# The last key block of a backward attention sweep, moved from beside a recurrent chain to between weight-gradient matmuls

## The chip, the cores and the metric

The kernel runs on one core of one Trainium2 chip. The metric is the device time of one execution in microseconds. Three runs of the kernel before gave a median of 5579.31 us (5578.82 to 5591.48).

## What is computed

The program is the forward pass and all gradients of a gated mix of two layers over 2048 tokens of width 576. Cut to what matters:

```python
g = sigmoid((x * gate_w).sum(-1))
# A: 32 query heads of 18 columns that share one key and one value head
p = softmax(q_h @ k.T * 18 ** -0.5);  a = concat(p @ v) @ wo
# B: 64 segments of 32 tokens; 8 memory rows go from one segment to the next
for s in range(64):
    h = concat([mem, x[32 * s:32 * s + 32]])
    q, k, v = h @ Wq, h @ Wk, h @ Wv            # 32 heads of 128 columns
    o = (masked_softmax(q @ k.T * 128 ** -0.5) @ v) @ Wo
    mem = o[:8];  out_B[s] = o[8:]
out = g * a + (1 - g) * out_B
# and the gradients of out in x, wq, wk, wv, wo, mem0, Wq, Wk, Wv, Wo and gate_w
```

The change concerns two parts of the backward pass: the gradients of A's one key and one value head, and B's recurrence run backward. It also concerns the weight gradients of B, which come after both. What is computed stays the same.

## The kernel before

The engines each run their own instructions in order and wait for each other through semaphores. Between the first stages and the end the order is the order of the code: `manual_schedule` is on, and two Python generators are woven by hand. `Kern.weave` runs a sweep and a chain side by side: a few leading sweep steps, then after every `yield` of the chain one sweep step, or more where the dictionary `extra` says so for the number of that yield. What follows is named **piece** for the stretch of chain between two yields, and **segment** for the chain's work on one of B's 64 segments.

**The sweep** (`a_pass2`) makes A's key and value gradients. It goes over 4 blocks of 512 keys (kb); for each over 16 pairs of heads and 16 tiles of 128 queries, so 256 steps a block, 1024 in all, each for one **pair** of heads. Step n issues:

- two matmuls for the scores of step n + 1 into `b_S` (two PSUM banks, one buffer of this kind), on 32 rows of TensorE each,
- two matmuls for dP of step n into two of three `b_dP` banks, on 32 other rows each,
- ACT's exponential of `b_S` into `b_E` (L1801), and DVE's product of `b_dP` and `b_E` into `b_dS` (L1824), in two halves,
- four matmuls of step n - 1 that add into `b_acc`, on 32 columns of TensorE each.

So `b_S` of the next step can be filled only after the exponential has read it. Queries come as `b_QS` from `qs_dram`, 256 KB for four steps (L1782), keys as `b_KV`, once a block. At a block's end ACT copies `b_acc` into a tile of the `b_dS` kind (L1837), and POOL stores it in `dkv_dram` (L1839).

**The chain** (`b_chain_bwd`) goes backward over the 64 segments. A segment depends on the one after it through `dm`, the gradient of the memory rows. Its 16 pieces are, in order: three for the projection of `dm` with WoT (two halves of 20 matmuls, 32 columns of TensorE each, into the banks `r_pj` and `r_x`); one for transposes (`mem_T`) and the dv gradient (`mem_grad`); one for the score gradients (`pd`, then `dS` on DVE); ten that share 48 `heads` **units** of four matmuls of 288 columns (`r_pj` from `WT` and `r_dT`), two of them with the other two `mem_grad` calls, and the last of them with the copies `r_hp` on ACT (L1167) and `r_hs` on DVE (L1168); and one for the row sums `pm`, which give the next `dm` (L1185).

Beside this, the chain makes B's dk and dv of the upper 11 of 16 token tiles in 176 **key/value units** (`kv_load`, `kv_mm`, `kv_out`): eight matmuls into `r_x`, a copy on ACT (L1035), a store on POOL (L1036). Four units ride in each of the 5th to the 48th segments, each copied one piece after its matmuls. `load_dT` (L973) reads such rows back, transposed, for later segments. Nearly all loads are issued by SP's queue, in the order of the code.

`weave` gives the sweep 12 leading steps and eight extra ones at each of the pieces 4, 7 and 10; with one step a piece for 16 x 64 = 1024 pieces the sweep ends in the 62nd segment, and the last two segments run alone.

**The weight gradients** (`b_dw`) come after `b_post`. `groups` yields groups of matmuls that contract over 20 tiles of 128 rows into `w_acc` (six PSUM banks): for k < 4 the output is dWo (pairs of accumulators of 288 columns), then dWq, dWk and dWv (512 columns). Copies alternate between DVE and ACT (L77, L79). Between the groups stand transposes of `mem_tok` (banks `z_pt`) and one `gate` for each k, with a row of DVE operations (L909 to L920).

Of the kernel before, what the change touches and what calls it, by code (L numbers as in the profile page):

```python
# [36 lines left out]
KVT = 11  # L37
RIDE = 24
# [8 lines left out]
class Kern:  # L47
# [529 lines left out]
    def mem_tok(self, wi, sp, psum, nb):  # L577
# [10 lines left out]
        for mt in range(n):  # L588
# [9 lines left out]
            for h8 in range(4):  # L598
                pt = psum.tile([P, 8, P], BF16, name="z_pt", bufs=nb)
# [298 lines left out]
    def gate(self, tt, L, wo, sp, psum):  # L898
# [3 lines left out]
        pa = [psum.tile([P, 512], F32, name="w_acc", bufs=6) for _ in range(2)]  # L902
# [27 lines left out]
    def b_chain_bwd(self, wot, sp, kd, kvp, keep, psum):  # L930
# [86 lines left out]
        def kv_mm(n):  # L1017
# [4 lines left out]
            pk = psum.tile([P, 4, P], F32, name="r_x", bufs=1)  # L1022
# [22 lines left out]
        for s in reversed(range(NSEG)):  # L1045
# [3 lines left out]
            n0 = 4 * (NSEG - 1 - s - 4)  # L1049
# [3 lines left out]
            pj = [psum.tile([P, 512], F32, name=nm, bufs=1) for nm in ("r_pj", "r_x")]  # L1053
            for k, parts in enumerate((((0, (0, 1, 2)),), ((0, (3, 4)), (1, (0,))), ((1, (1, 2, 3, 4)),))):
                for j, kts in parts:
                    self.proj_part(pj[j], d_, self.WoT, j, kts)
                    if kts[-1] == 4:
                        self.evac(dOm[:, 4 * j:4 * j + 4, :].rearrange("p u e -> p (u e)"), pj[j][:], use="s")
                if k == 1:
                    x_rows(s, 0, pT[:, 0, :])  # L1060
                yield
# [24 lines left out]
            pg = mem_grad("r_pj", ((rows(mrow["dx"], E), [perm] * 8), (rows(dOm), blk(PqB))))  # L1086
            yield
# [14 lines left out]
            mem_cols(2, pg)  # L1102
# [3 lines left out]
            self.expand(dSB[:], dS[:].rearrange("p a (u q) -> p (a u) q", q=8), 16)  # L1106
            yield
# [12 lines left out]
            heads(2)  # L1120
            kv_mm(n0)
# [4 lines left out]
            kv_out(n0)  # L1126
# [12 lines left out]
            yield  # L1139
            heads(2)  # L1140
            kv_mm(n0 + 1)
            nc.gpsimd.dma_start(self.dTm_dram[s // 16][:, :, s % 16, :], dTc[:].rearrange("p w u c t -> p w (u c t)"))
            yield
            kv_out(n0 + 1)
            heads(7)
            load_dT(s - 1, 2)
            if s:
                pad_in("p", nxt["pT"][:, 1, :])
            yield
            heads(7)  # L1150
            if s:
                load_c(s - 1)
            yield
            heads(2)
            kv_mm(n0 + 2)
            if s:
                Pq = pad_T("p")
            yield
            kv_out(n0 + 2)
            heads(7)  # L1160
            load_dT(s - 1, 0)
            if n0 == -4:
                kv_load(0)
            yield
            heads(7)
# [4 lines left out]
            if n0 == -4:  # L1170
                kv_load(1)
# [3 lines left out]
            kv_mm(n0 + 3)  # L1175
# [137 lines left out]
    def b_dw(self, sp, wA, wB, wH, psum):  # L1313
# [3 lines left out]
        WS = ("o", "dq", "dk", "dv")  # L1317

# [24 lines left out]
        def groups(k, ts, ht):  # L1343
            if k < 4:
                od = self.outs[10].rearrange("h e d -> (h e) d")
                for t, cs in ts:
                    for i in range(4):
                        acc = [psum.tile([P, 512], F32, name="w_acc", bufs=6) for _ in range(2)]
                        for it in range(n):
                            for hf in range(2):  # L1350
                                self.mm(acc[hf][:, 0:288], lhsT=t[:, it, 128 * i:128 * i + 128],
                                        rhs=ht[:, it, 288 * hf:288 * hf + 288], start=(it == 0), stop=(it == n - 1))
                        o16 = sp.tile([P, D], BF16, name="w_o16b", bufs=3)
                        for hf in range(2):
                            self.evac(o16[:, 288 * hf:288 * hf + 288], acc[hf][:, 0:288])
# [5 lines left out]
            for t, cs in ts:  # L1361
                for kt in range(4):
                    acc = psum.tile([P, 512], F32, name="w_acc", bufs=6)
# [7 lines left out]
            acc = psum.tile([P, 512], F32, name="w_acc", bufs=6)  # L1371
# [10 lines left out]
        with self.tc.manual_schedule():  # L1382
# [6 lines left out]
            mem = None  # L1389
            for k in range(16):  # L1390
                ts = nxt
                if k % 4 == 0 and k < 12:
                    mem = self.mem_tok(k // 4, sp, psum, 2)
                    next(mem)
# [5 lines left out]
                if k == 15:  # L1400
                    self.final_load(wA, wH)
# [7 lines left out]
            pg = [psum.tile([P, 512], F32, name="w_acc", bufs=6) for _ in range(2)]  # L1409
# [354 lines left out]
    def a_pass2(self, keep, sp, psum):  # L1764
# [4 lines left out]
        def load_KV(kb):  # L1769
            if kb < 4:  # L1770
                KV[kb] = keep.tile([P, 512], BF16, name="b_KV", bufs=2)
                nc.sync.dma_start(KV[kb][:], self.kv_dram[:, kb * 512:kb * 512 + 512])

        load_KV(0)
        Q, S, E_, D_ = {}, {}, {}, {}
        NC = 4 * NPR * NTT // 4

        def load(c):
            if c < NC:
                p, q4 = (c // 4) % NPR, c % 4  # L1780
                QS = sp.tile([P, 2, 512], BF16, name="b_QS", bufs=3)
                nc.sync.dma_start(QS[:], self.qs_dram[p, q4])  # L1782
                Q[c] = (QS[:, 0, :], QS[:, 1, :].rearrange("p (a b) -> p a b", b=P))

        def pair(n):
            return n // (NPR * NTT), n // 4, n % 4
# [22 lines left out]
        NP_ = 4 * NS  # L1809
        for n in range(NP_ + 1):  # L1810
            if n < NP_:
                if n % 4 == 2:
                    load(n // 4 + 2)
                if n % NS == NS // 2:
                    load_KV(n // NS + 1)
                if n + 1 < NP_:
                    mm_S(n + 1)
                dP = [psum.tile([P, 512], F32, name="b_dP", bufs=3) for _ in range(2)]
# [6 lines left out]
            if n > 0:  # L1825
# [9 lines left out]
                if o % NS == NS - 1:  # L1835
                    dkv = sp.tile([P, 2, 512], BF16, name="b_dS", bufs=2)
                    nc.scalar.copy(dkv[:, 0, :], acc[:])  # L1837
                    k0 = (o // NS) * 512
# [266 lines left out]
```

## Time and profile before

| what | value |
| --- | --- |
| median of 3 runs | 5579.31 us |
| span of the profiled execution | 5569.0 us, 204829 instructions |
| median less span (no time of the profiled execution alone is recorded) | 10.3 us |
| PE / DVE / ACT / POOL busy | 94% / 67% / 63% / 41% |
| chain and sweep together, first to last r_hp and the lead | 2814.1 to 4523.4 us |
| `b_post` up to the wait ahead of the weight gradients | about 4525 to 4774 us |
| weight gradients | 4788.6 to about 5466 us |
| final stage | about 5470 to 5569 us |

Times in the profile are in us unless marked ns. PE is TensorE's matmuls, PEld its weight loads, DVE VectorE, ACT ScalarE, POOL GpSimd, SP SyncE. A row of a timeline has the start from the span's beginning, the time from the first start to the last end, engine, line, operation, output and input, how many in a row, and in brackets the idle time before and who ended it. A row of the windows view has the stretch, its length, the busy time of PE, PEld, DVE, ACT and POOL with instruction counts, the granted TensorE clock (1.00 is full), the busy share of the 16 DMA engines, and GB/s. A row of the waits view has the engine, what waited and for whom, the total, how many times, and the longest. Ends of matmuls are modelled, so two matmuls that run together or follow each other closely both show about 0.39 us; their starts are the better measure. The helper `mm` is L82, so matmuls are told apart by their tiles.

### The profile page before, as it was taken

To read this page: it belongs to the slowest core of one execution; us is meant where nothing else is said; L and a number is where in the kernel's file an instruction comes from. 1 tells how busy PE (TensorE), PEld (TensorE's weight loads), DVE (VectorE), ACT (ScalarE), POOL (GpSimd) and SP (SyncE) were. 2 spreads that over 40 slices of the span, in tenths; PEclk is the share of its full clock that TensorE was granted. 3 is DMA by queue.
4 is the path that set the end of the run, shared out by engine and by line. 5 is a ranking of instruction groups with operands and counts; after the bars stand their busy time and mean duration, and the time that the engine had idled before them with its cause. 6 is when DMAs were issued, how large, how long until landed. Compare 5 with 4: busy or idle time off the path is not lost. (4 is left out here: it accounts for less than half of the span.)

```text
span 5569.0 us, 204829 instructions
## 1 busy us (share of the span) xinstructions
PE 5231.2 (94%) x87117; PEld 2909.5 (52%) x87117; DVE 3726.0 (67%) x6818; ACT 3506.8 (63%) x5266; POOL 2297.4 (41%) x4320
## 2 busy tenths in 40 slices
PE   7999999999999998999969999999998889899999
PEld 6434444444444445777734555555544457674444
DVE  5337888888888887888868888888888821121111
ACT  4327888788878886888857878878877732111101
POOL 4004555555555545555514544444543421122213
PEclk9999999999999998999979999999999999999999
DMA  6646666766675546888765999999987679876653
GB/s 214 220 173 136 136 138 137 137 138 133 144 135 117 119 99 192 258 256 253 233 228 156 199 200 208 213 202 212 215 181 146 138 181 250 244 214 229 209 165 115
DMA packets 1109896, 1012.49 MB, mean 182 GB/s; under 512 B 666386, under 2 KB 919067, under 8 KB 1099378
## 3 DMA queue, kind: packets, MB, share of 16 engines
q1 hardware_dynamic: 1004706, 747.39, 56.4%
q0 software_dynamic: 100736, 247.10, 14.4%
q8 instruction: 681, 11.16, 0.9%
q10 hardware_dynamic: 3536, 4.90, 0.3%
q14 instruction: 237, 1.94, 0.1%
HBM read 547.90 MB, written 383.13 MB: 167 GB/s over the span
## 5 line engine op out<-in xcount | busy, mean ns | idle before, releaser
L1684 DVE TENSOR_TENSOR a_W<-a_dP,a_E 128x512 bf16<-128x512 f32 x2048 | 1315.1, 684 | 269.9 <-issue 128.7
L1824 DVE TENSOR_TENSOR b_dS<-b_dP,b_E 128x512 bf16<-128x512 f32 x2048 | 1311.8, 684 | 249.3 <-issue 109.0
L1801 ACT ACTIVATE b_E<-b_S 128x1024 bf16<-128x1024 f32 x1024 | 1048.3, 1024 | 308.2 <-PE b_dP L82 237.0
L1654 ACT ACTIVATE a_E<-a_S 128x1024 bf16<-128x1024 f32 x1024 | 1050.0, 1025 | 255.8 <-PE a_dP L82 166.5
L82 PEld LDWEIGHTS <-b_QS 32*128 32x128 bf16 (+1 forms) x8192 | 258.0, 92 | 564.9 <-issue 521.4
L82 PE MATMUL r_pj<-WT,r_dT 128*32 128x288 bf16 x12288 | 496.7, 289 | 17.0 <-issue 16.5
L82 PE MATMUL b_S<-b_KV,b_QS 32*128 32x512 bf16 x2048 | 409.1, 390 | 96.8 <-ACT b_E L1801 77.7
L82 PE MATMUL w_acc<-w_d,w_h 128*128 128x512 bf16 (+1 forms) x2400 | 473.8, 379 | 0.0
L82 PE MATMUL a_S<-a_QD,l_KV 32*128 32x512 bf16 x2048 | 400.3, 384 | 39.5 <-ACT a_E L1654 34.9
L82 PE MATMUL b_acc<-b_dS,b_QS 128*32 128x512 bf16 x2048 | 430.8, 399 | 0.7 <-DVE b_dS L1824 0.5
L82 PE MATMUL b_dP<-b_KV,b_QS 32*128 32x512 bf16 x2048 | 409.8, 394 | 8.2 <-DVE b_dS L1824 8.2
L82 PE MATMUL a_acc<-a_W,l_WK 128*32 128x512 bf16 x4096 | 414.5, 390 | 2.7 <-issue 2.4
L82 PE MATMUL b_acc<-b_E,b_QS 128*32 128x512 bf16 x2048 | 412.8, 400 | 0.0
L82 PE MATMUL a_acc<-a_E,l_VK 128*32 128x512 bf16 x4096 | 405.0, 381 | 5.8 <-issue 1.1
L82 PE MATMUL a_dP<-a_QD,l_KV 32*128 32x512 bf16 x2048 | 399.2, 386 | 0.0
L82 PEld LDWEIGHTS <-r_dT 128*32 128x32 bf16 x12288 | 333.8, 97 | 114.8 <-issue 24.0
L82 PEld LDWEIGHTS <-w_h 128*128 128x128 bf16 (+1 forms) x2688 | 229.8, 100 | 258.8 <-issue 6.9
L82 PEld LDWEIGHTS <-hm 128*32 128x32 bf16 x7680 | 203.9, 97 | 195.0 <-issue 0.8
L769 POOL TENSOR_TENSOR x_P<-x_E,x_r 128x512 bf16<-128x512 bf16 x128 | 152.7, 1193 | 293.6 <-DVE x_r L766 293.6
L79 ACT CAST w_o<-w_acc 128x512 bf16<-128x512 f32 x54 | 31.6, 585 | 384.3 <-PE w_acc L82 365.0
L77 DVE CAST w_o<-w_acc 128x512 bf16<-128x512 f32 x54 | 37.3, 691 | 333.4 <-PE w_acc L82 306.5
L82 PEld LDWEIGHTS <-l_KV 32*128 32x128 bf16 x4096 | 122.0, 91 | 250.6 <-issue 206.2
(461 smaller groups left out, 10953.2 us busy)
## 6 DMA issues: line engine op xcount, KB each, us to landing
b_QS<-qs_dram SPq DMA_DIRECT2D x256, 256.0 KB
dOx_dram<-p_tok SPq DMA_DIRECT2D x16, 1024.0 KB
c_vx<-vx_dram SPq DMA_DIRECT2D x64, 256.0 KB
krow_dram<-c_k POOLq DMA_DIRECT2D x64, 256.0 KB
qrow_dram<-c_q POOLq DMA_DIRECT2D x64, 256.0 KB
vrow_dram<-c_v POOLq DMA_DIRECT2D x64, 256.0 KB
x_q<-qx_dram SPq DMA_DIRECT2D x32, 512.0 KB
x_dO<-dOx_dram SPq DMA_DIRECT2D x32, 512.0 KB
```

Of the source, the lines that this page charges most:

```text
L77: nc.vector.tensor_copy(out, in_)
L79: nc.scalar.copy(out, in_)
L82: return self.nc.tensor.matmul(out, lhsT, rhs, start=start, stop=stop, tile_position=tp, skip_group_check=True)
L769: nc.gpsimd.tensor_tensor(out=o[:, r, :], in0=Et[:, :, lo:lo + n], in1=rl[:].unsqueeze(2).to_broadcast([P, 4, n]), op=ALU.mult)
L1654: nc.scalar.activation(E_[n][:], S.pop(n)[:], ACT.Exp, scale=SCALEA)
L1684: nc.vector.tensor_tensor(out=W_[n][:, i, :], in0=dP[i][:], in1=E_[n][:, i, :], op=ALU.mult)
L1801: nc.scalar.activation(E_[n][:], S.pop(n)[:], ACT.Exp, scale=SCALEA)
L1824: nc.vector.tensor_tensor(out=D_[n][:, i, :], in0=dP[i][:], in1=E_[n][:, i, :], op=ALU.mult)
```

## The change

- The sweep is cut. Key blocks 0 to 2 (768 steps) stay beside the chain. Block 3 becomes a second generator in `b_dw`: six steps ahead of all groups, then one step whenever `weave` there has counted 4800 more columns of `w_acc` matmuls, inside the groups; what is left would be run at k = 15. This second sweep has pools of its own, two `b_dP` banks in place of three, and its loads go out on ACT's queue.
- `w_acc` has three banks in place of six, and `z_pt` shares them. For k < 4 the two halves of an output are made one after the other.
- The chain has 12 pieces a segment in place of 16. The projection is in two pieces of a whole half each; the score gradients, the heads and the loads are spread anew.
- Key/value units: four in each of the 5th to 16th segments, then three up to the 59th. The first of a segment stands behind the score gradients in bank `r_pj`, with its copy in the same piece; the others are copied in the same piece too, but for the last.
- `extra` gives eight more steps at the pieces 4, 6 and 7, and one fewer, that is none, at the first piece of each of the 5th to 40th segments. Lead, pieces and extras make 768 steps.
- The block-end copy uses a tile of the units' kind (`r_kvo`) in place of a `b_dS` tile.

```diff
+        def kv_first(s):
+            q = NSEG - 1 - s - 4
+            return 4 * q if q < KV4 else 4 * KV4 + 3 * (q - KV4)      # KV4 = 12
...
-            for k, parts in enumerate((((0, (0, 1, 2)),), ((0, (3, 4)), (1, (0,))), ((1, (1, 2, 3, 4)),))):
...
+            for j, nm in enumerate(("r_pj", "r_x")):
+                pj = psum.tile([P, 512], F32, name=nm, bufs=1)
+                self.proj_part(pj, d_, self.WoT, j, range(NKT))
+                self.evac(dOm[:, 4 * j:4 * j + 4, :].rearrange("p u e -> p (u e)"), pj[:], use="s")
...
             self.expand(dSB[:], dS[:].rearrange("p a (u q) -> p (a u) q", q=8), 16)
+            kv_mm(n0, "r_pj")
+            kv_out(n0)
             yield
...
-            heads(2)
-            kv_mm(n0)
+            heads(4)
+            kv_mm(n0 + 1)
...
-            kv_out(n0)
+            kv_out(n0 + 1)
             heads(8)
...
-            heads(3)
+            heads(4)
+            load_dT(s - 1, 2)
             mem_cols(0, mem_grad("r_x", ((rows(L["kx"]), blk(dSB)), (rows(mrow["k"]), blk(dSB, 8)))))
             yield
-            heads(3)
             mem_cols(1, mem_grad("r_x", ((rows(mrow["dx"]), [perm] * 8), (rows(mrow["q"]), blk(dSqB)))))
+            heads(5)
...
+            heads(9)
             if s:
                 load_c(s - 1)
+                pad_in("p", nxt["pT"][:, 1, :])
+            yield
+            heads(9)
+            load_dT(s - 1, 0)
+            if n1 - n0 == 4:
+                kv_mm(n0 + 2)
+                kv_out(n0 + 2)
...
+            heads(9)
             hp = sp.tile([64, 2 * GD], F32, name="r_hp", tag="r_dSB", bufs=1)
...
-            kv_mm(n0 + 3)
+            kv_mm(n1 - 1)
...
     def b_dw(...):
+        def weave(c):
+            cols[0] += c
+            if cols[0] >= WCOLS:                                       # WCOLS = 4800
+                cols[0] -= WCOLS
+                next(sweep, None)
...
                     for it in range(n):
                         self.mm(acc[:], lhsT=ht[:, it, kt * P:kt * P + P], rhs=t[:, it, :],
                                 start=(it == 0), stop=(it == n - 1))
+                        weave(512)
...
+            for _ in range(6):
+                next(sweep)
             for k in range(16):
...
     build_full:
-                k.weave(k.b_chain_bwd(...), k.a_pass2(a3k, a3s, a3p), 12, ((4, 8), (7, 8), (10, 8)),
+                extra = {4: 8, 6: 8, 7: 8}
+                extra.update({12 * q: -1 for q in range(4, 40)})
+                k.weave(k.b_chain_bwd(...), k.a_pass2(a3k, a3s, a3p, 0, 3, nc.sync, rv, 3), 12, extra,
...
-                k.b_dw(ws, wA, wB, wH, wp_)
+            with SB("a4s") as a4s, PS("a4p") as a4p, PS("wp") as wp_:
+                k.b_dw(ws, wA, wB, wH, wp_, k.a_pass2(a4s, a4s, a4p, 3, 4, nc.scalar, a4s, 2))
```

More of the change, by code (lines that the diff above doesn't have):

```diff
@@ L598, in mem_tok @@
             for h8 in range(4):
-                pt = psum.tile([P, 8, P], BF16, name="z_pt", bufs=nb)
+                pt = psum.tile([P, 8, P], BF16, name="z_pt", tag="w_acc", bufs=3)
                 for u in range(8):
@@ L901, in gate @@
         diff = sp.tile([P, D], F32, name="o_diff", bufs=1)
-        pa = [psum.tile([P, 512], F32, name="w_acc", bufs=6) for _ in range(2)]
+        pa = [psum.tile([P, 512], F32, name="w_acc", bufs=3) for _ in range(2)]
         for kt in range(NKT):
@@ L1021, in kv_mm @@
             a, b = kvl.pop(n)
-            pk = psum.tile([P, 4, P], F32, name="r_x", bufs=1)
+            pk = psum.tile([P, 4, P], F32, name=bank, bufs=1)
             for i in range(4):
@@ L1362, in groups @@
                 for kt in range(4):
-                    acc = psum.tile([P, 512], F32, name="w_acc", bufs=6)
+                    acc = psum.tile([P, 512], F32, name="w_acc", bufs=3)
                     for it in range(n):
@@ L1370, in groups @@
                     yield
-            acc = psum.tile([P, 512], F32, name="w_acc", bufs=6)
+            acc = psum.tile([P, 512], F32, name="w_acc", bufs=3)
             for it in range(n):
@@ L1400, in b_dw @@
                 if k == 15:
+                    for _ in sweep:
+                        pass
                     self.final_load(wA, wH)
@@ L1408, in b_dw @@
             nc.vector.tensor_copy(dz16[:], self.dz_all[:])
-            pg = [psum.tile([P, 512], F32, name="w_acc", bufs=6) for _ in range(2)]
+            pg = [psum.tile([P, 512], F32, name="w_acc", bufs=3) for _ in range(2)]
             for tt in range(NTT):
@@ L1814, in a_pass2 @@
                 if n % NS == NS // 2:
-                    load_KV(n // NS + 1)
+                    load_KV(kb0 + n // NS + 1)
                 if n + 1 < NP_:
                     mm_S(n + 1)
-                dP = [psum.tile([P, 512], F32, name="b_dP", bufs=3) for _ in range(2)]
+                dP = [psum.tile([P, 512], F32, name="b_dP", bufs=nd) for _ in range(2)]
                 mm_u([t[:] for t in dP], n, 64)
```

85 lines of the change are left out of this document (33 added, 52 removed).

## The prediction

> **What bounds the kernel now.** I read the page first. Its engine shares hide the stages, so I asked next for the windows of the stage that the change touches, then the timelines inside it, then the waits.
>
> The backward chain runs with the sweep from 2814 to 4523 us. The starts of r_hp (one per segment, L1167) mark the segments: the first lies at 2906.7, the fourth at 2982.4, the 48th at 4135.0, the 61st at 4464.2, the last at 4523.4. The windows between them:
>
> ```profile
> core 0: us, PE busy (x) PEld busy (x) DVE busy (x) ACT busy (x) POOL busy (x), PEclk, DMA share, GB/s
> 2814.10:2906.70 92.60, 65.57 (x761) 23.32 (x760) 68.14 (x112) 54.53 (x58) 9.79 (x18) 0.64 0.73 241
> ...
> 2982.40:4135.00 1152.60, 1106.75 (x23184) 595.99 (x23180) 964.62 (x1673) 928.53 (x1235) 555.21 (x1014) 0.99 0.92 204
> 4135.00:4464.20 329.20, 294.62 (x6447) 155.53 (x6443) 284.42 (x495) 249.52 (x313) 134.71 (x248) 1.00 0.68 144
> 4464.20:4523.40 59.20, 47.97 (x1215) 29.93 (x1211) 22.89 (x46) 23.17 (x38) 31.30 (x57) 0.94 0.62 116
> ```
>
> A segment without key/value units takes 329.2 / 13 = 25.3 us. One with four units and no stall takes the same (3506.3 to 3531.5 is 25.2), although PE does more in it. So PE's work does not set the pace. ACT's timeline shows what does:
>
> ```profile
> 4458.34 1.02 ACT L1801 ACTIVATE b_E<-b_S 128x1024 bf16<-128x1024 f32 x1 [0.53 <-PE b_dP L82]
> 4459.89 1.02 ACT L1801 ACTIVATE b_E<-b_S 128x1024 bf16<-128x1024 f32 x1 [0.53 <-PE b_dP L82]
> 4461.44 1.02 ACT L1801 ACTIVATE b_E<-b_S 128x1024 bf16<-128x1024 f32 x1 [0.53 <-PE b_dP L82]
> ```
>
> The exponentials start 1.55 us apart: 1.02 of ACT, then 0.53 in which PE must refill the only b_S tile. This **ring** of 16 pairs makes 16 x 1.55 = 24.8 of the 25.2 us. Inside one turn PE does this:
>
> ```profile
> 3916.58 0.39 PE L82 MATMUL b_S<-b_KV,b_QS 32*128 32x512 bf16 x2
> ...
> 3916.91 0.39 PE L82 MATMUL b_acc<-b_dS,b_QS 128*32 128x512 bf16 x2
> ...
> 3917.13 1.03 PE L82 MATMUL r_pj<-WT,r_dT 128*32 128x288 bf16 x28
> 3918.14 0.39 PE L82 MATMUL b_S<-b_KV,b_QS 32*128 32x512 bf16 x2
> ```
>
> The pair holds PE for 0.55 us before a chain matmul can start, seven head units (four matmuls each) follow at 0.125 us, and the next b_S needs 0.22 after the last unit's start: 0.55 + 6 x 0.125 + 0.22 = 1.52, just inside 1.55. Eight units should take 1.65, and the piece with eight does (exponentials at 4450.20 and 4451.84). PE is thus nearly full in segments with units, and with fewer pairs per segment PE becomes the bound.
>
> The weight-gradient stage (4788 to 5466) is PE's already: after one wait at its start (PE's timeline) it is 0.99 busy at clock 0.99, while DVE and ACT are nearly free (the window):
>
> ```profile
> 4788.58 12.11 PE L82 MATMUL w_acc<-w_h,w_d 128*128 128x288 bf16 x80 [14.17 <-DMA w_d<-ox_dram]
> ```
>
> ```profile
> 4800.00:5470.00 670.00, 662.49 (x4165) 370.46 (x4164) 117.71 (x234) 68.23 (x109) 148.88 (x242) 0.99 0.70 215
> ```
>
> **The change, part by part.** The instruction counts of PE, DVE and POOL stay as they are; 65 load issues go from SP's queue to ACT's. So the sum is one stage against another, in us of the profiled execution.
>
> *Chain stage, per segment.* Prices, from starts in the PE timeline: a piece with n head units 0.65 + 0.125n; a projection half (five groups of 0.216) 0.55 + 4 x 0.216 + 0.31 = 1.73; a unit after heads 0.63 (0.22 to switch, 0.48 for its eight matmuls, 0.15 out, in place of the 0.22 out of the heads). A piece costs the larger of this and 1.55. The twelve pieces with three units: halves 1.73 + 1.73; transposes and first gradient 1.60; score gradients (PE at 1.36) with a unit 2.11; four heads and a unit 1.78, taken as 1.90, since the heads now share bank r_pj with a unit whose ACT copy (0.58) ends after the pair (bounds 1.78 and 2.03); eight heads 1.70; four heads and a gradient 1.67; gradient and five heads 1.94; three times nine heads 5.31; unit and row sums 1.60. Sum **21.3**. Where the sweep step is left out the two halves share one pair (2.80 for 3.46): 20.6, with four units 21.25. Without units (pieces 4, 5 and 12 at or near 1.55) 20.35.
>
> What else moves costs nothing of its own: the gradient copy of piece 4 goes one piece up, beside work that PE does anyway; the loads keep their order on SP's queue, which loses the query loads of 256 pairs (0.5 to 1.1 an issue) and so waits less. The shortest lead is that of the last r_dT load, issued at a segment's end for unit 32 of the next: 13 pieces or 20 us before, ten pieces or 17 us now; what it may cost is in the stalls.
>
> The first segment keeps 12 leading pairs and 24 extra ones at clock 0.64 and loses four pairs: 92.6 to 86. Then 3 x 20.35 + 12 x 21.25 + 24 x 20.6 + 19 x 21.3 + 5 x 20.35 = 1317; together 1403.
>
> *Stalls.* The 44 segments with units take 1152.6, at 25.2 each 1109. Of the 44 us over, 16 are three segments at block ends, whose output copy borrowed a b_dS tile; that tile is no longer borrowed. The other 28 (0.65 a segment) come with a DMA share near 1; the waits name part of them:
>
> ```profile
> PE b_S L82 <- ACT b_E L1801: 17.1, 92, 0.4
> PE r_pj L82 <- issue: 13.5, 10, 2.6
> PE b_dP L82 <- DVE b_dS L1824: 8.2, 3, 2.9
> ```
>
> The transfers are now to be had in fewer microseconds, so I take 1.3 for 55 segments, 72 us (bounds: 36, and the rival below). Stage after: 1403 + 72 = 1475, before 4523.4 - 2814.1 = 1709: **-234**.
>
> *Weight-gradient stage.* Of the last 257 sweep steps six stand ahead, 251 between matmuls, one per 4800 columns. No row has a b_S after a w_acc. Nearest rows: two 512-column w_acc start 0.216 apart, but 0.309 where the second one uses 64-column tiles; b_S to b_acc is 0.33; b_acc to a 128-row matmul 0.32 to 0.33. A pair costs (0.309 - 0.216) + 0.33 + 0.33 = 0.75, in all 188.
>
> The Trainium skill, TensorEngine Tiling, Tiling Modes (Key Properties), says that a change of tiling mode drains TensorE; the 0.309 against 0.216 agrees, and this speaks against the change, which adds three mode changes a pair. Without drains two times 0.216 would make it 108 instead of 188.
>
> The ring is covered there: 4800 columns are 2.0 us, a turn is 2.75, more than 1.55 and, with three dP banks cut to two, than the 0.5 and 1.29 until DVE has freed it. Without that cover each pair would cost the ring (rival below). DVE's gate work (about 3.3 us in a row, 16 times) can hold b_dS and then b_acc behind it: 8 us (0 to 25). Three w_acc banks instead of six are filled again after at least 2.4 us, copies take 0.4 to 1.0: 4 (0 to 10). The six leading pairs (1.77 each when alone) and their load lie beside the 14.17 us wait for w_d: 3 (0 to 11). The loads on ACT's queue stand behind exponentials that are long over: nothing (at 0.6 an issue, 39 if ACT were short). Sum **+203** (bounds 185 to 235).
>
> Net -31: span 5538, and from the median, 10.3 us above the span, **5548 us**. A measurement of this kernel can tell about 0.3% (17 us) from no change.
>
> **Rivals.**
> 1. *DMA takes the bound (slower).* Four units with 16 pairs keep the engines at share 0.99:
>
> ```profile
> 3008.80:3109.80 101.00, 99.17 (x2112) 53.81 (x2108) 87.34 (x152) 84.23 (x112) 50.39 (x92) 1.00 0.71 181
> 3506.30:3607.00 100.70, 98.57 (x2107) 53.65 (x2103) 87.51 (x153) 84.16 (x112) 50.38 (x92) 1.00 0.99 209
> 4135.00:4236.00 101.00, 90.59 (x1985) 47.96 (x1984) 87.35 (x153) 77.05 (x97) 41.85 (x77) 1.00 0.69 149
> ```
>
> That is 24.9 us of packet time a segment; a unit is (0.99 - 0.69) x 25.2 / 4 = 1.9; a query load of 256 KB at 204 / 0.92 GB/s is 1.2. The new segments need 23.4 (four units), 21.5 and 21.8, more than their 21.25, 20.6 and 21.3 of PE. If no more than the 0.92 that the stage averaged is to be had, they take 25.4, 23.4 and 23.7: 1317 against my 1226, hence **5639**. It decides once the share that can be had is under about 1.0. For it: the stalls lie where the share is high. Against: the second window ran at 0.99 at the ring's pace, so packet times overlap.
> 2. *Nothing more is lost, the stalls keep their rate* and the gate hides: 1439 + 192, **5501**.
> 3. *Woven pairs pay the ring*: an exponential or b_dS queued behind copies exposes 1.55 a pair, +200: **5748**. Against: the turn of 2.75.
> 4. *The segment doesn't shrink*, because the chain's own latency binds: segments without a sweep take 17.1 and 17.7; if every pair added its 0.65 to that, 12 would make 25.2, and only the cost is left: **5782**. Against: 16 pairs would then make 28, and it is 25.2.
>
> **How the numbers follow.** Chances: forecast 0.52 (5515 to 5580; 0.37 of it below 5562, 0.15 within), rival 1 0.17 (0.02 within), rival 2 0.19, rival 3 0.08, rival 4 0.04. Faster 0.56, within 0.3% 0.17, slower 0.27. The range 5500 to 5640 leaves out rivals 3 and 4 and the ends of 1 and 2.
>
> **What would show it.** r_hp starts 20.5 to 22.5 us apart; exponentials in the chain stage no longer at 1.55 but at 1.7 to 2.1, with ACT idle up and PE's wait for b_E near nothing; in the weight-gradient stage b_S about 2.75 us apart, DVE near 0.55 busy, the stage about 200 us longer. Wrong would be: segments of 24 us at a share near 1 (rival 1), b_S 3.5 us apart there (rival 3), r_hp still 25 us apart (rival 4).

## The result, and the profile after

The changed kernel takes 5630.49 us (median of 4 runs, 5621.96 to 5640.52), the kernel before 5579.07 beside it: a ratio of 1.009, 95% interval 1.0073 to 1.0107. It is slower by 51 us; the forecast was 5548, and its rival 1 gave 5639. The profiled execution spans 5638.8 us (its own time is 5640.52). Stage by stage, from the starts and ends of the same instructions in both traces, in us:

| stage | before | after | change | forecast |
|---|---|---|---|---|
| up to the first b_E (no code of it changed) | 2814.1 | 2827.0 | +12.9 | 0 |
| first b_E to last r_hp (chain stage) | 1709.3 | 1547.4 | -161.9 | -234 |
| to the first y_pk | 13.2 | 18.7 | +5.5 | 0 |
| b_post | 237.8 | 244.7 | +6.9 | 0 |
| to the first w_acc | 14.2 | 22.8 | +8.6 | +3 |
| first to last w_acc | 684.9 | 879.2 | +194.3 | +200 |
| from there to the end | 95.6 | 99.0 | +3.4 | 0 |

The two profiled executions are 69.8 us apart, the medians 51: the profile after shows the slowest of its four executions. The +12.9 is no effect of the change: the code up to the first b_E is the same in all kernels of this case, it takes 2814 to 2839 us in their profiles, and the profile of before has the shortest time. b_post takes 234 to 242 us in all the other profiles. (The last w_acc before ends at 5473.4, not at the 5466 that stands ahead; the table goes by 5473.4.) So the step that failed is the chain stage, and there is no other of its size. Its windows in the profile after (first segment; three without units; the 55 with units; five without; and the weight-gradient stage):

```profile
core 0: us, PE busy (x) PEld busy (x) DVE busy (x) ACT busy (x) POOL busy (x), PEclk, DMA share, GB/s
2827.00:2915.90 88.90, 62.80 (x729) 22.82 (x728) 63.34 (x104) 50.48 (x53) 9.83 (x18) 0.62 0.77 249
2915.90:2977.90 62.00, 58.84 (x1393) 32.87 (x1392) 50.48 (x90) 44.88 (x60) 31.08 (x57) 1.00 0.49 120
2977.90:4270.90 1293.00, 1214.98 (x26589) 686.24 (x26585) 884.73 (x1578) 878.00 (x1242) 674.66 (x1223) 0.95 1.00 200
4270.90:4374.40 103.50, 98.10 (x2319) 54.95 (x2315) 83.67 (x149) 74.88 (x101) 51.56 (x94) 1.00 0.70 145
4660.60:5539.80 879.20, 863.15 (x6190) 410.88 (x6260) 434.81 (x738) 320.38 (x361) 148.56 (x244) 0.99 0.61 184
```

Where there are no units (second and fourth row) a segment takes 20.7 us, close to the forecast 20.35. In the third row the DMA share is 1.00, the granted clock is down to 0.95, and a segment takes 23.5 us where 21.0 without stalls and 22.3 with them were forecast. PE's list of waits for that window says what stalls it:

```profile
PE r_x L84 <- issue: 18.6, 16, 2.4
PE r_x L84 <- DMA r_kr<-dOx_dram: 10.4, 6, 2.5
PE r_pj L84 <- DMA r_kr<-dOx_dram: 8.4, 6, 2.1
PE b_S L84 <- ACT b_E L1811: 8.1, 44, 0.4
PE b_S L84 <- DMA b_QS<-qs_dram: 7.9, 12, 1.7
PE r_pj L84 <- DMA r_dx<-dmx_dram: 4.4, 6, 1.2
```

The ring has gone, as forecast: b_S waits for b_E only 8.1 us. In its place stand loads that are late (r_kr, b_QS, r_dx) and "issue". Before, the transfers of the same stage were late by less than 2 us in all.

In the weight-gradient stage PE's timeline shows the woven pair as it was priced:

```profile
4899.82 0.39 PE L84 MATMUL b_S<-b_KV,b_QS 32*128 32x512 bf16 x2
...
4900.15 0.39 PE L84 MATMUL b_acc<-b_dS,b_QS 128*32 128x512 bf16 x2
...
4900.48 2.33 PE L84 MATMUL w_acc<-w_d,w_h 128*128 128x512 bf16 x10
4902.74 0.39 PE L84 MATMUL b_S<-b_KV,b_QS 32*128 32x512 bf16 x2
```

From b_S to the next w_acc are 0.66 us, and ten w_acc with the switch to b_S after them take 2.26 where ten alone take 2.16: 0.76 in all, forecast 0.75. PE is 0.98 busy there; nothing waits for the ring.

### The profile page after: what moved, and what is told of

Same layout as the page of the kernel before. It is cut to its first block, busy times and chain, and to the rows that moved or that the text cites. A ratio compares the mean times of both kernels' runs of the same rounds, so it can differ in the third digit from the quotient of the medians.

```text
span 5638.8 us, 204625 instructions
## 1 busy us (share of the span) xinstructions
PE 5276.0 (94%) x86911; PEld 2898.0 (51%) x87117; DVE 3729.1 (66%) x6818; ACT 3503.1 (62%) x5266; POOL 2305.2 (41%) x4320
## 5 line engine op out<-in xcount | busy, mean ns | idle before, releaser
L84 PEld LDWEIGHTS <-b_QS 32*128 32x128 bf16 (+1 forms) x8192 | 232.2, 92 | 600.3 <-issue 541.7
L84 PE MATMUL w_acc<-w_d,w_h 128*128 128x512 bf16 (+1 forms) x2327 | 494.2, 381 | 7.5 <-issue 5.6
L84 PE MATMUL r_pj<-WT,r_dT 128*32 128x288 bf16 x12288 | 480.6, 296 | 2.3 <-issue 1.2
L84 PEld LDWEIGHTS <-w_h 128*128 128x128 bf16 (+1 forms) x2688 | 217.0, 100 | 258.8 <-issue 47.0
L771 POOL TENSOR_TENSOR x_P<-x_E,x_r 128x512 bf16<-128x512 bf16 x128 | 152.7, 1193 | 291.9 <-DVE x_r L768 289.4
L1375 POOL DMA_DIRECT2D out_dram<-w_o x96 | 52.2, 544 | 452.4 <-DVE w_o L79 240.3
L84 PEld LDWEIGHTS <-l_WK 128*32 128x32 bf16 x4096 | 106.9, 93 | 223.1 <-issue 222.8
```

The lines of the kernel that those rows point to most:

```text
L84: return self.nc.tensor.matmul(out, lhsT, rhs, start=start, stop=stop, tile_position=tp, skip_group_check=True)
L771: nc.gpsimd.tensor_tensor(out=o[:, r, :], in0=Et[:, :, lo:lo + n], in1=rl[:].unsqueeze(2).to_broadcast([P, 4, n]), op=ALU.mult)
L1375: nc.gpsimd.dma_start(od[kt * P:kt * P + P, cs], o16[:])
```

## The experiments

Times are medians; the ratio is to the kernel before, run on the same chip in the same rounds (its medians: 5581 to 5589). "Segments" are the 55 from the fourth r_hp to the 59th. My theory 1 is that the DMA engines are full there; its rivals are that the units' loads are asked for too late (2), that the pieces are dearer than priced (3), and, from the second round on, that SP's queue is too long (4).

**Prices first: the woven block.** *block3_out* takes the sweep out of b_dw:

```
-                k.b_dw(ws, wA, wB, wH, wp_, k.a_pass2(a4s, a4s, a4p, 3, 4, nc.scalar, a4s, 2))
+                k.b_dw(ws, wA, wB, wH, wp_, no_block(a4s))     # writes zeros once
```

> The changed kernel with the fourth key block left out of the weight-gradient stage (its dk and dv are written as zeros; the six pairs ahead of the first matmul go too). It prices the woven block: forecast 203 us, and the profile of the changed kernel shows 194 between first and last w_acc and some 8 ahead of it. All theories: the chain stage stays at 1547 +- 10; whole kernel 5630 - 200 = 5415 to 5435 if the price is additive; if the block also costs through what lies beside it (three banks for w_acc, gate work), it would be below 5405.

5443.1 us (0.9738, 0.9721 to 0.9755). First to last w_acc is back at 685.7, the chain stage stays (segments 1293.0), and the wait ahead of the first w_acc falls from 22.8 to 15.2. The block costs 193.5 + 7.6 = 201 us there; the forecast said 203. The whole kernel's ratio falls by 0.0352 against the changed kernel's 1.0090, some 197 us. This half was right.

**Is it the transfers?** Two runs leave transfers out and every matmul in:

```
-            if 0 <= s < NSEG - KR:          # transposes_out: load_dT does nothing
+            if s < 0:
```
```
-            a = kvp.tile(...); nc.sync.dma_start(a[:], ...)      # unit_loads_out
-            b = kvp.tile(...); nc.sync.dma_start(b[:]..., ...)
-            kvl[n] = (a, b)
+            kvl[n] = kvz                    # two tiles set to zero once
```

> The changed kernel with the three transposed loads per segment into r_dT left out (256 KB each; what they add to the chain is left out, the matmuls that read r_dT stay). Theory 1 (DMA engines full): these are some 7 of 21 to 23 us packet time of a segment, so the share falls to about 0.7 and the waits for r_kr, b_QS, r_dx and 'issue' go: 55 segments with units in 1185 to 1210 us instead of 1293, whole kernel about 5530 to 5545. Theory 2 (loads of units asked for too late): the waits for r_kr stay, 5610 to 5630. Theory 3 (pieces dearer): 5620 to 5640.

> The changed kernel with the two big loads of every key/value unit left out (r_ks and r_kr, 128 KB each; the units' matmuls, copies and stores stay and multiply zeros, so dk and dv of the tokens are not the reference's). In the changed kernel the 55 segments with units take 1293 us between r_hp and r_hp, of which I work out 1182 for their pieces without a stall, and the DMA share there is 0.95 to 1.02. Theory 1 (the DMA engines are full): 3.2 units x 256 KB of some 4.7 MB a segment go, the share falls to about 0.85, and not only the waits for r_kr but also those for b_QS, r_dx and the 'issue' waits go: 55 segments in 1195 to 1215 us, whole kernel about 5540. Theory 2 (the loads of a unit are asked for too late, two units ahead, since the units now stand in neighbouring pieces): only the waits for r_kr go (19 us in the list of waits): whole kernel 5605 to 5615. Theory 3 (the pieces themselves are dearer than I priced: banks, copies, late instructions): no change, 5625 to 5640.

5526.5 us (0.9893, 0.9878 to 0.9908) and 5558.5 us (0.9944, 0.9927 to 0.9961). The windows of the segments, transposes_out and then unit_loads_out:

```profile
2974.80:4167.40 1192.60, 1169.29 (x26589) 669.72 (x26585) 880.22 (x1578) 875.03 (x1243) 671.78 (x1223) 1.00 0.72 184
```
```profile
2989.90:4210.00 1220.10, 1187.06 (x26589) 676.09 (x26585) 882.52 (x1578) 876.65 (x1242) 671.95 (x1223) 0.98 0.83 174
```

With the same instructions on PE the segments take 1193 and 1220 us instead of 1293, at a share of 0.72 and 0.83, and the clock goes back to 1.00 and 0.98. The waits for "issue" and b_QS, which have no part in the loads taken out, go too (transposes_out: 1.6 and 0.2 us left). So the 100 us hang on the transfers. Which property of them costs the time is not told by these two runs: with the loads, SP's work of issuing them goes too.

**Late because they start late?** *units_apart* moves the second unit three pieces on (below, cut to the heads), *one_more_ahead* loads r_kr three units ahead instead of two, in four buffers:

```
-            heads(4); kv_mm(n0 + 1)         # units_apart: heads 8, 8, 4, 5, 5+unit, 9, 9
+            heads(8)
...
-            heads(9)
+            heads(5); kv_mm(n0 + 1); kv_out(n0 + 1)
```

> The changed kernel with the second unit of a segment moved three pieces later (behind five of the nine head steps of the sixth heads' piece; heads 8, 8, 4, 5, 5, 9, 9), so that the loads of the next unit have about 4 pieces everywhere, with no byte more or less. Theory 1 (DMA engines full): the waits move to others, whole kernel 5620 to 5640. Theory 2 (asked for too late): most of the 19 us of r_kr waits go: 5605 to 5615.

> The changed kernel with r_kr loaded three units ahead instead of two (four buffers instead of three; r_xq0 and r_xq1 share one buffer to make room), no byte more or less and no piece moved. Theory 1 (DMA engines full): no change or below 10 us, 5620 to 5635. Theory 2 (asked for too late): the 19 us of r_kr waits go, 5605 to 5615, as with the units apart.

5607.4 (1.0030, 1.0016 to 1.0044) and 5631.8 (1.0083, 1.0064 to 1.0102). The units apart gain 23 us by the medians and 0.6% by the ratios, which theory 2 expected, but not as it expected: the sum of PE's waits stays (69.8 us in the changed kernel, 69.1 here), with r_kr still 19.3 of it. What shrinks is the time at half clock (below); the segments take 1269 us:

```profile
2977.70:4247.10 1269.40, 1192.12 (x26589) 677.64 (x26585) 888.73 (x1578) 878.34 (x1243) 671.25 (x1223) 0.98 0.96 203
```

One more ahead gains nothing: r_kr is in time, and r_ks (15.5 us), still two ahead, is late instead.

**Late because SP's queue is long?** First a run with fewer bytes, in more loads:

```
-            nc.sync.dma_start(mrow["k"][:]..., self.row_dram["k"][s])        # r_q likewise
+            for c in range(0, P, 32):
+                nc.sync.dma_start(mrow["k"][c:c + 8]..., self.row_dram["k"][s][c:c + 8])
```

> The changed kernel with the loads of r_k and r_q cut to the rows that are multiplied by something other than zero (8 of every 32 partitions: four pieces of 16 KB instead of one of 256 KB, for each of the two), nothing else: 384 KB of some 4.7 MB a segment go, none of them a load of a unit and none a transposed one. Theory 1 (the DMA engines are full): a third of what leaving out the transposes gave, 55 segments with units in 1250 to 1270 us instead of 1293, whole kernel 5590 to 5610. Theory 2 (only the units' loads come late): 5620 to 5640.

5688.8 us (1.0199, 1.0176 to 1.0222): the wrong side of both theories. The share falls to 0.78, and the segments grow to 1349:

```profile
2979.60:4328.40 1348.80, 1239.95 (x26589) 695.92 (x26585) 884.05 (x1578) 879.36 (x1242) 671.51 (x1223) 0.93 0.78 176
```

SP's timeline in this run has the reason at the last line:

```profile
3318.21 0.61 SPq L963 DMA_DIRECT2D r_kx<-kx_dram  x1
3318.92 1.61 SPq L966 DMA_DIRECT2D r_k<-krow_dram  x4
3320.63 0.31 SPq L969 DMA_DIRECT2D r_dx<-dmx_dram  x1
3321.04 4.11 SPq L972 DMA_DIRECT2D r_q<-qrow_dram  x3
```

and SP's list of waits sums it:

```profile
SPq L972 <- DMA r_kx<-kx_dram: 144.3, 54, 3.8
```

r_q does not use r_kx. In the trace's records SP's loads take eight completion semaphores strictly in turn, which suggests that a load goes out only when the one eight places ahead has landed. Eight small loads now stand where two large ones stood; the third of r_q stands eight places behind r_kx, and SP, with b_QS and the units' loads behind it, waits 2.7 us a segment for r_kx. The same edit makes the kernel before slower too (*before_fewer_bytes*):

> The kernel before with r_k and r_q cut to 8 of 32 rows. Its 44 segments with units and transposes took 1152.6 us, some 1124 without the stalls that I count (0.65 us a segment), at a share of 0.92 to 0.99. Theory 1 (it too ran close to full): it gains a part of these 28 us, 5565 to 5580. If it was not bound by the DMA engines anywhere: 5575 to 5590, no change.

5604.8 us (1.0039, 1.0024 to 1.0054), b_QS late by 25.5 us. And with the two helpful edits beside it (*all_three*) the loss stays:

> The changed kernel with the second unit three pieces later, r_kr three units ahead, and r_k and r_q cut to 8 of 32 rows. If fewer bytes and an earlier start add up: 55 segments in 1225 to 1245 us, whole kernel 5560 to 5580, that is 0.1 to 0.5% faster than the kernel before. If they mend the same stalls: about as the better of the two, 5595 to 5605.

5670.4 us (1.0156, 1.0138 to 1.0174). So SP's queue can be made the bound. Whether it is the bound of the changed kernel, the next four ask. Three let POOL issue some of the loads and keep every byte (*both_on_pool_apart* is the first two together with the second unit moved). *half_the_rows* halves the r_k and r_q loads and keeps their number; it leaves the memory rows of the other half out of the gradients:

```
-                nc.sync.dma_start(kvS[rg]..., ...)          # unit_heads_on_pool (kvR likewise)
+                nc.gpsimd.dma_start(kvS[rg]..., ...)
-      k.a_pass2(a3k, a3s, a3p, 0, 3, nc.sync, rv, 3)         # query_loads_on_pool
+      k.a_pass2(a3k, a3s, a3p, 0, 3, nc.gpsimd, rv, 3)
-            nc.sync.dma_start(mrow["k"][:]..., ...[s])       # half_the_rows (r_q likewise)
+            nc.sync.dma_start(mrow["k"][0:64]..., ...[s][0:64])
```

> The changed kernel with the three small loads that every second unit needs (r_kvS 64 KB, r_kvR twice 32 KB; 4.8 a segment) issued by POOL instead of SP; no byte more or less. What the runs so far leave: theory 1 (the DMA engines are full) is contradicted by the run with fewer bytes in more loads, in which the DMA share fell from 1.00 to 0.78 and the time rose by 56 us. New theory 4 (SP's queue is the bound: its 25 loads a segment go one behind the other, SP needs 19.3 of a segment's 23.6 us for them in its records, and waits between them): 20 loads a segment are left on SP, 2.9 us less of SP's time, and the waits for r_kr, b_QS, r_dx shrink: 55 segments with units in 1215 to 1250 us instead of 1293, whole kernel 5560 to 5590. Theory 1: no change, 5620 to 5640. POOL is busy for 675 of 1293 us, these loads would add some 160; if that is too much, its copies come late and it gets slower, over 5640.

> The changed kernel with the loads of b_QS and b_KV in the chain stage issued by POOL instead of SP (2.8 a segment of 256 KB), no byte more or less. Theory 4 (SP's queue): 2.8 loads and 1.6 us of SP's time a segment less, and b_QS no longer stands behind a unit's loads: 55 segments in 1240 to 1270 us, whole kernel 5585 to 5615. Theory 1 (DMA engines full): no change, 5620 to 5640.

> The changed kernel with r_kvS, r_kvR, b_QS and b_KV loaded by POOL's queue and the second unit of a segment three pieces later. Theory 4: 17 loads a segment are left on SP, near to the 18.5 of the run without the big unit loads, with nothing left out: 55 segments in 1195 to 1230 us, whole kernel 5535 to 5570, that is 0.2 to 0.8% faster than the kernel before. Theory 1: as with the units apart alone, 5600 to 5615.

> The changed kernel with the loads of r_k and r_q cut to the first 64 of 128 partitions (the memory rows of the other 64 are left out of the gradients), so 256 KB of some 4.7 MB a segment go and the number of loads stays. Theory 1 (DMA engines full): a quarter to a third of what the transposes gave, 55 segments in 1260 to 1275 us instead of 1293, whole kernel 5600 to 5615. Theory 4 (SP's queue, by the number of loads and the time they take to issue): 0 to 10 us less, 5620 to 5640.

5632.0 (1.0084, 1.0064 to 1.0104), 5654.1 (1.0122, 1.0099 to 1.0145), 5686.4 (1.0176, 1.0153 to 1.0198) and 5611.0 us (1.0038, 1.0023 to 1.0053). None of the first three comes near the times of theory 4. PE's waits in unit_heads_on_pool show why moving loads is no help:

```profile
PE r_pj L84 <- issue: 19.2, 13, 3.3
PE b_dP L84 <- DVE b_dS L1834: 14.8, 29, 1.4
PE r_x L84 <- issue: 13.2, 18, 1.8
```

The 20 us for the units' loads and the 8 for b_QS are gone, as theory 4 would have it, but "issue" has grown from 25 to 42 us and b_dP waits 15: the sum is 70 again, at the same share of 1.00. POOL has got the loads and is busy for 824 us of these segments instead of 675, so these runs alone do not clear SP's queue. half_the_rows adds no load to another engine. Its 5611 us lie in the range of theory 1 (5600 to 5615) and outside that of theory 4, and its ratio is 0.5% below the changed kernel's, for 256 KB a segment less. Its segments are only 11 us shorter where theory 1 expected 18 to 33, in a profile of the slowest of its ten executions (5627 us). That speaks for the bytes, by one run.

**What a stall costs.** This is the profile after, PE's timeline at a stall and then the windows ahead of, in and behind the stretch that follows:

```profile
3145.04 0.36 PE L84 MATMUL r_x<-r_dOT,r_vmT 128*8 128x8 bf16 x25
3146.95 0.20 PE L84 MATMUL r_x<-r_dOT,r_vmT 128*8 128x8 bf16 x7 [1.55 <-issue]
...
3147.95 0.55 PE L84 MATMUL r_pj<-r_kr,r_ks 128*128 128x128 bf16 x4 [0.40 <-DMA r_kr<-dOx_dram]
3148.87 0.60 PE L84 MATMUL b_S<-b_KV,b_QS 32*128 32x512 bf16 x2 [0.37 <-DMA b_QS<-qs_dram]
...
3149.42 0.61 PE L84 MATMUL b_acc<-b_dS,b_QS 128*32 128x512 bf16 x2
```
```profile
3144.00:3148.00 4.00, 2.05 (x90) 1.30 (x87) 1.58 (x3) 1.40 (x2) 3.87 (x8) 1.00 0.91 242
3148.00:3154.80 6.80, 6.34 (x76) 3.07 (x75) 3.05 (x6) 3.11 (x4) 1.77 (x4) 0.50 1.13 226
3154.80:3162.00 7.20, 7.20 (x180) 4.28 (x172) 5.03 (x8) 4.68 (x6) 3.47 (x7) 1.00 1.11 202
```

Two things are to be seen. The "issue" stall falls between the 25th and the 26th of 32 equal matmuls, so it is no operand that is late. PE's own instructions come by DMA: the trace has 681 packets of 16 KB on one instruction queue and 174,247 instructions of PE, so 256 a packet. Counted in the order of the trace, 26 of the 29 "issue" waits in these segments stand at one place of a block of 256 or at the place beside it, and in unit_heads_on_pool all 42 such waits do (at another place; some matmul records are missing from the trace after, which shifts the count). So these are waits for the next block of instructions. At each of the 12 over 0.9 us a packet ends 1.3 to 1.7 us before PE goes on. The packet takes 1.0 to 1.2 us there, like the others (median 1.1): it is not slow, but starts when PE has only 1 to 138 instructions left in its block (median of all packets 178). Why it starts so late is not shown. The Trainium skill (Runtime: NRT & Kernel Launch, Instruction fetch mechanics) says that blocks of 256 instructions are fetched ahead and that this is mostly hidden; the trace agrees where the DMA share is 0.72 (1.6 us of it), not at 1.00 (25 us).

And after the stall the granted clock is 0.50 for 6.8 us, in which b_S to b_acc takes 0.55 instead of 0.33. The clock's records show such stretches of 3.4 us or a multiple: 119 us in the segments after, 34 in the same stage before. The Trainium skill (TensorE: Matmul & The Clock Gate, HAM oscillation) puts this down to idle gaps over some 3.4 us; here no gap in these segments is longer than 2.5 us, so the measurement decides. 20 of the 21 stretches have a gap of 0.5 to 2.5 us at their start or ending in the 2.4 us ahead of it; of the 31 gaps of 0.9 us or more, six stand near no such stretch. So a gap of this size often brings half clock, not always: with equal sums of waits (70, 69 and 70 us) the changed kernel, units_apart and unit_heads_on_pool have 119, 58 and 68 us of it.

From units_apart, where the waits are the same, the half-clock time is 58 instead of 119 us and the segments 24 us shorter: 0.39 us lost per us at half clock, a price fitted to this one pair of profiles. With that, and 1173 us for the pieces (transposes_out less its 15.5 of waits and 4 for 10 us of half clock), the segments of the other runs can be summed:

| run | share | waits | at half clock | 1173 + waits + 0.39 x half | measured |
|---|---|---|---|---|---|
| after | 1.00 | 70 | 119 | 1289 | 1293 |
| unit_loads_out | 0.83 | 25 | 51 | 1218 | 1220 |
| half_the_rows | 0.99 | 62 | 106 | 1276 | 1282 |
| one_more_ahead | 0.98 | 74 | 113 | 1291 | 1296 |
| query_loads_on_pool | 0.99 | 74 | 154 | 1307 | 1309 |
| fewer_bytes | 0.78 | 101 | 191 | 1348 | 1349 |
| unit_heads_on_pool | 1.00 | 70 | 68 | 1270 | 1299 |

Only the last stands out (both_on_pool_apart, by 22 us, does too): what POOL's longer queue costs beyond waits and clock was not found.

**Did the kernel before have room?** *before_transposes_out* is the edit of transposes_out in the kernel before, and *before_units_spread* is the change's unit schedule alone, in the sixteen pieces:

```
-            n0 = 4 * (NSEG - 1 - s - 4)
+            n0, n1 = kv_first(s), kv_first(s - 1)     # third unit only if n1 - n0 == 4, last one n1 - 1
```

> The kernel before with the three transposed loads per segment into r_dT left out (their part of the chain is left out). Theory 1 says that before had little room too (share 0.92): 25 of its 42 us of waits and some 10 us at half clock go, 5545 to 5565. If its waits were of another kind: 5575 to 5590.

> The kernel before with the second of the change's edits alone: the units four per segment for twelve segments and then three per segment, at the kernel before's places, so over 55 instead of 44 segments; sixteen pieces and all four key blocks in the chain stage as before. The units' own work is the same and only moves, so without stalls nothing changes; the transposing segments carry 0.8 unit or 1.5 us of packet time less each, so a part of the 42 us of waits there goes: 5560 to 5580. If spreading costs by itself (11 more segments with copies in the way): over 5590.

5562.8 us (0.9957, 0.9942 to 0.9972) and 5586.7 us (0.9998, 0.9985 to 1.0012). The kernel before loses 24 us of its 44 segments to the transposed loads (1152.6 to 1128.2), a quarter of what the changed one loses. Spreading its units alone does nothing; neither of the two ranges expected it.

**How many pairs belong in the chain stage?** Where the pieces' time goes to stalls anyway, a pair in every piece may be free. *twelve_all_paired* is units_apart with a pair in the 36 pieces that had none, *paired_not_apart* the same without the moved unit, *fourteen_pieces* cuts the heads into nine pieces, also with the second unit moved. The fourth block is split and its two parts are added; the pairs left over are woven in every 5400 columns, every 12800 with fourteen pieces:

```
-                extra.update({12 * q: -1 for q in range(4, 40)})
-                ... k.a_pass2(a3k, a3s, a3p, 0, 3, nc.sync, rv, 3)
+                ... k.a_pass2(a3k, a3s, a3p, 0, 800, nc.sync, rv, 3)       # in pairs; 928 with fourteen pieces
...
-  k.a_pass2(a4s, a4s, a4p, 3, 4, nc.scalar, a4s, 2)
+  k.a_pass2(a4s, a4s, a4p, 800, 1024, nc.scalar, a4s, 2)
```

> The changed kernel with the chain cut into fourteen pieces (heads 6, 6, 4, 4, 4, 6, 6, 6, 6; the second unit beside the fifth of them), a pair in every piece, so that 160 of the 256 pairs of the fourth key block run in the chain stage too and 96 between weight-gradient matmuls (one every 12800 columns, two ahead); the two partial sums are added at the end. Theory 1 (the segments' time is set by what the DMA engines must carry, 23 to 24 us a segment): the 55 segments grow only from 23.5 to some 24 us (+30 us), the other nine by 1.4 us each, and the weight-gradient stage shrinks by 160 x 0.775 = 124 us less some us: 5535 to 5570, 0.3 to 0.8% faster than the kernel before. If the pieces themselves are the bound (0.8 us for each more, stalls as before): 25.1 us a segment, 5600 to 5615.

> The changed kernel with the second unit three pieces later, a pair in every piece (the 36 pieces without one get one), so that 32 pairs of the fourth block run in the chain stage and 224 between weight-gradient matmuls. From the run with the units apart (5607): 36 pairs at 0.5 us more in the chain, or nothing where the DMA engines set the time, against 32 x 0.775 = 25 us less later: 5580 to 5600.

> The changed kernel with a pair in every piece and 224 pairs between weight-gradient matmuls, but with the second unit where the change has it. If the two edits of twelve_all_paired add (apart gave 23 us, paired then 39): 5585 to 5600, with the 55 segments near 1285 to 1300 us. If the pairs take time from the segments here (0.5 us each, 18 us): 5600 to 5615.

> The same kernel as twelve_all_paired on another occasion (5568, ratio 0.9978): 5560 to 5580, ratio to the kernel before 0.996 to 1.000.

5592.1 (1.0009, 0.9996 to 1.0022), **5568.1 (0.9978, 0.9962 to 0.9994)**, 5593.2 (1.0006, 0.9990 to 1.0022) and, measured again, **5570.4 (0.9974, 0.9961 to 0.9987)**. Windows of the segments with fourteen pieces, and of segments and weight-gradient stage with twelve all paired:

```profile
2984.70:4343.70 1359.00, 1285.04 (x27753) 713.51 (x27750) 1067.57 (x1870) 1021.96 (x1389) 670.72 (x1224) 0.99 0.89 197
```
```profile
2978.40:4239.80 1261.40, 1205.23 (x26877) 681.15 (x26873) 934.50 (x1650) 910.09 (x1278) 670.68 (x1223) 0.99 0.95 207
4607.80:5463.00 855.20, 840.50 (x5949) 407.50 (x6020) 397.63 (x677) 289.20 (x329) 148.65 (x244) 0.99 0.62 189
```

The 36 pairs do not lengthen the chain stage (1261 against 1269 with the unit moved, 1289 against 1293 without), and the stage that they left is 21 to 28 us shorter; waits ahead of b_post and of w_acc shrink by 5 to 7 us each, for a reason that stays open. twelve_all_paired is 0.2 to 0.3% faster than the kernel before, and 12 us faster than the range expected. Fourteen pieces are not: two more pieces a segment cost 98 us for 110 pairs, 0.89 each, so theory 1, taken as "pairs beside the transfers are free", holds only up to a full set of twelve.

## Why the prediction was wrong

- *The ring sets the pace before; PE is next.* Right: PE is 0.94 busy in the segments, and the wait for b_E is near nothing.
- *Weight-gradient stage +203.* Right in size: 201 measured by leaving the block out. Its main term was right too (251 pairs at 0.76 are 191, forecast 188). For gate work and banks some 3 us are left where 12 were forecast, and ahead of the first w_acc it is 7.6 where it was 3.
- *First segment 86, segments without units 20.35.* 88.9 and 20.7: nearly right.
- *Pieces of the segments with units: 1154 us without stalls.* 1173 in the run that has almost none. Of the sum's terms, the projection was mis-sized: from b_S to b_S in PE's timeline (medians) it takes 3.22 us with one pair against 2.80, and 3.77 with two against 3.46, in all 21 us over 36 and 19 segments. A pair there costs PE 0.55 us, so the 36 that were put back cost some 20. They came out free because the waits fell from 69 to 48 us and the time at half clock from 58 to 38 us.
- *Stalls: 72 us (bounds 36 and rival 1).* **The step that failed.** 1293 - 1173 = 120 us: 70 of waits, some 46 of half clock by the fitted price, and 4 that neither explains. The forecast doubled before's rate per segment. It held the window at share 0.99 and the ring's pace as a sign that a full share costs nothing, and it had no term for the clock.
- *Rival 1 (DMA takes the bound, 5639).* Close in time (1317 us for the segments, 1293 measured; 5639 against 5630), and right in its engine; not in its mechanism. Its sign, segments of 24 us at a share near 1, came (23.5 at 1.00). But the share did not stop at 0.92; it went to 1.00. What costs is that there PE waits up to 2.5 us for single loads and for its next instructions, and that it then often runs at half clock. That the totals are so close is in part luck: the rival's segments are 24 us too long, and what the profile after has beside the two stages makes up for it.
- *Net -31.* The chain stage gave 162 us for 256 pairs, 0.63 each, where 0.91 was forecast; a woven pair costs 0.79 with all that goes with it. In the same 44 segments sixteen pieces with spread units take 1147 us, fourteen 1094, twelve all paired 1017: a pair taken out saves 0.60 at first and 0.88 then (one profile each; from sixteen to fourteen the second unit and the block-end copy change as well). The change sits near break-even, and the stalls tipped it.
- *10.3 us between span and median.* In the profile after it is 1.7; with 1.7 the profiled execution of before took some 5571 us, less than any of the four measured.

Shown by runs: the price of the block, that the loss hangs on the transfers, that r_kr's lead is not its cause, and that pairs in the empty pieces do not lengthen the stage. Shown by the order of the trace: that the "issue" stalls are waits for the next block of instructions. Argued, not tried by itself: the price of half clock, the eight-load window on SP, and that it is the bytes and not SP's queue, for which half_the_rows is the only run that adds no work elsewhere. Open: why instruction packets start late, and why r_kx lands so late. The Trainium skill (DMA: Bandwidth & Descriptors, Rules for kernel authors) says that a transfer whose outermost dimension is smaller than 16 is confined to at most that many engines; r_kx's source begins with a dimension of four. No run here shows which engines carry it, and a reordered load wasn't tried.

## What to carry to other kernels

Before work is moved from a stage that hides it to one that doesn't, compare the price of the last piece moved with what taking it out saves there, and look at the DMA share that the shortened stage will have: transfers that fitted at 0.92 came late at 1.00, and a stall of a microsecond or two on TensorE can be paid again at half clock. When waits for one load are mended and the sum of the waits stays the same, look for the limit in what the loads share. Fewer bytes in more loads can be slower, as in fewer_bytes, where SP waited 2.7 us a segment between the small loads.

## What the runs showed of the hardware

- Idle gaps of 0.5 to 2.5 us on PE stood at or just ahead of 20 of the 21 stretches of 3.4 to 13.7 us at a granted clock of 0.50; some 0.39 us of the stage was lost per us of them, by a fit to one pair of profiles.
- At a DMA share of 1.00 PE stalled at the edges of its blocks of 256 instructions, 25 us in 1293, and 42 us in the run where it waited for no load; at 0.72 it was 1.6 us.
- An ordinary load holds SP for 0.3 to 0.7 us (medians by load), a transposed one into r_dT for 1.3 and more (medians of 1.27 to 1.77). In fewer_bytes SP waited 144 us at r_q for r_kx, the load eight places ahead, which r_q does not use.
